# Rows of wo beside the values: sums, parts and loads in another order; one load ahead of stores at the end

## The chip, the cores and the metric

The kernel runs on one core of one Trainium2 chip. The metric is the time of one execution in device microseconds, taken as the median of several runs. A profile is one execution recorded by the hardware profiler; its times are counted from the start of its span. The engines are PE (matmul; its weight loads are PEld), DVE (vector), ACT (scalar), POOL (GpSimd) and SP, which here only issues transfers. An engine works through its instructions in order, and an instruction that waits holds up those behind it on that engine.

## The reference

The output is a blend of two blocks on the same input x of 2048 x 1024, with a gate from x:

```python
g = sigmoid((x * gate_w).sum(-1, keepdims=True))
a = attention(x, wqkv, wo)        # 32 heads of 32, softmax, then @ wo
b = peer(x, w_q, k1, k2, u, v)    # 32 heads; each token's best of 64 experts, gelu, @ v
return g * a + (1 - g) * b
```

Everything is float32.

## The kernel before, in words

The work is one long program in an order written by hand (`manual_schedule`): the tile framework adds the waits that data and buffers need, and nothing is moved. Matrix products of 128x512 are made with operands split into a high and a low part (ACT makes the high part by a copy, DVE the low part by a subtraction; `split`, lines 98 and 99), three matmuls for each product of parts. The large ones save one eighth of the matmuls: a product of 2x2 blocks is made from seven products P1 to P7 of sums of blocks (class `Halves`), whose results DVE adds.

The stages, one after the other: queries and keys (to about 360 us), the router of the second block, the values, attention of 32 heads, and the product with wo. The change touches the seam between values and attention, and the last stage.

**The values.** `values_unit(u)` for u = 0 to 6 makes 256 rows of the values by seven products (line 987), in 19 us. P1 is followed by a copy on ACT; after P6 DVE makes four additions (`combine`, line 916), after P2, P3 and P4 one each. The four sums that come out are stored to the DRAM tensors VD[0] and VD[1] (named vd), from where attention loads its V. While unit u runs, ACT and DVE make all factors of unit u + 1. The products use fixed banks of PSUM. In the last unit the order is P1, P7, P5, P6, P3, P2, P4, and between P2 and P4 PE makes the first eight score matmuls of attention (`first_scores`, line 1278) into the banks 5, 6, 7, 0, 1, 2, 5, 6; bank 2 holds P3 until DVE has added it.

**The rows of wo beside them.** In the units 3 to 6 (i = 0 to 3) four combinations T1 to T4 of blocks of wo are made for the last stage. `load_early(i)` loads four pieces of 128x512 into `early` (named xl in the profile), on POOL's queue. `sums_early` makes the four combinations in place, with four operations on DVE. `split_early(i, j)` makes the parts of combination j (the low part in place) and stores both to TD (t0h, t0l and so on), on POOL's queue. The pieces of i + 1 go into the same places, so a load has to wait until the low part there is stored. Before, the sums came after P7 (k == 1), the parts after P5 (k == 2: j = 0, 1) and after P6 (k == 3: j = 2, 3), each behind that product's own operations, and behind them the four loads.

**The queues.** Transfers are issued by SP, ACT or POOL, whose rows carry the line of the helper `dma` (L80). In the last unit, three of the stores to VD were on SP's queue and one (from P4) on POOL's. Behind them SP issues `load_v`, four transfers that bring V of the first four heads, and then K and Q of head 1.

**Attention.** For every two tiles of keys PE makes eight score matmuls (line 1385) and then two tiles' products with V (line 1406). Z holds K and Q of head 0; two rows of its K are set to 1 by a memset on DVE (line 1293), before in unit 3.

**The last stage.** The first chunk of 256 rows is made plainly (`wo_mm`, line 1622), the others by seven products each, in `unit(n)`. `plain_out` copies the plain chunk's four banks to SBUF and stores them, on SP's queue. `load_t(3, ...)` loads T4, a factor of P4, in eight transfers into the right halves of the tiles woh and wol, also on SP's queue.

Of the kernel before, what the change touches and what calls it, by code (L numbers as in the profile page):

```python
# [17 lines left out]
D = 1024  # L18
H = 32
KC = D // 128  # L20
HC = KC // 2
# [10 lines left out]
def gated_mha_peer_kernel(ctx, tc, xT, wqkv, wv, wo, wq, k12, ug, v, out):  # L32
# [8 lines left out]
    nc = tc.nc  # L41
# [10 lines left out]
    VD = [dram.tile([S, 512], F32, name=f"vd{i}") for i in range(2)]  # L52
# [3 lines left out]
    wo_rows = wo.rearrange("(j d) m -> d j m", j=4)  # L56
# [21 lines left out]
    def dma(dst, src, queue=nc.sync):  # L78
        a, b = (ap.bitcast(F32) if ap.dtype == F32R else ap for ap in (dst, src))
        return queue.dma_start(a, b)  # L80
# [190 lines left out]
    def load_kq(h, tiles):  # L271
        for t, which in zip(tiles, (1, 0)):
            src = QKD[which][32 * h:32 * h + 32]
            dma(t[:32, :], src[:, QK_PARTS[which][0], :])
            dma(t[32:96, :], src.rearrange("d a s -> (d a) s"))

    def load_shift(h, tiles):
        dma(tiles[1][96:98, :], SHD[h])
# [636 lines left out]
    def tt(out, a, b, op=OP.add):  # L915
        nc.vector.tensor_tensor(out=out, in0=a, in1=b, op=op)  # L916
# [12 lines left out]
    def load_x_raw(u):  # L929
        dma(x_raw[u % 2], xT[:, u * W:(u + 1) * W].rearrange("(k p) m -> p k m", p=128))  # L930
# [146 lines left out]
    def peer_turn(Ahl):  # L1077
        for n in range(NQ):
            pt = bank_at((5, 0, 1, 7)[n])
            for t in range(4):  # L1080
                nc.tensor.transpose(pt[:, t * 128:(t + 1) * 128],
                                    Ahl[:, 4 * n + t, :].bitcast(F32), ident)
            at = Z[0][:, n * 512:(n + 1) * 512]
            nc.scalar.activation(at, pt, AF.Copy)
            dma(ATD[:, n * 512:(n + 1) * 512], at)
# [64 lines left out]
    early = more[:, :4]  # L1150
    for k, name in enumerate(("S1", "S3", "th0", "th1")):
        work[name] = more[:, 4 + k]

    def load_early(i):
        for j in range(4):
            c0 = (i + j // 2 * HC) * D + j % 2 * 512
            dma(early[:, j], wo_rows[:, :, c0:c0 + 512], nc.gpsimd)

    def sums_early():
        b11, b12, b21, b22 = (early[:, j] for j in range(4))  # L1160
        tt(b11, b12, b11, OP.subtract)
        tt(b12, b22, b12, OP.subtract)
        tt(b22, b22, b11, OP.subtract)
        tt(b21, b21, b22, OP.subtract)

    def split_early(i, j):
        hi, lo = work[f"th{j}"].bitcast(F32R), early[:, j].bitcast(F32R)
        split(hi, lo, early[:, j])
        for part, t in enumerate((hi, lo)):

            dma(TD[(0, 2, 3, 1)[j]][part][:, i, :], t, nc.gpsimd)

    load_early(0)
    NU = (NT - 2) // 2
    pso = None
    peer = {}
# [10 lines left out]
    def values_unit(u):  # L1187
        last = u == NU - 1
        c1, u2, u3, u5 = (work[k] for k in ("c1", "u2", "u3", "u5"))
        if last:  # L1190
            free = x_raw[(u + 1) % 2].rearrange("p k m -> p (k m)").rearrange("p (a m) -> p a m", m=512)
            c1, u2, u3, u5 = (free[:, k] for k in range(4))
        order = (("P1", "P2", "P3", "P7", "P5", "P6", "P4") if u == 0 else
                 ("P1", "P7", "P5", "P6", "P3", "P2", "P4") if last else
                 ("P1", "P7", "P5", "P6", "P2", "P3", "P4"))
        bank_no[0] = 6 if u else 7
        p, done = {}, set()

        def out(j, half, t, queue=nc.sync):
            dma(VD[half][(2 * u + j) * 128:(2 * u + j + 1) * 128, :], t, queue)  # L1200

        def combine(name):
            if name == "P6":
                tt(u2, c1, p["P6"])
                tt(u3, u2, p["P7"])
                tt(u2, u2, p["P5"])
                tt(u5, u3, p["P5"])
                out(1, 1, u5)
            if "P6" in p:
                if "P2" in p and "C11" not in p:  # L1210
                    p["C11"] = tt(c1, c1, p["P2"])
                    out(0, 0, c1)
                if "P3" in p and "C12" not in p:
                    p["C12"] = tt(u2, u2, p["P3"])
                    out(0, 1, u2)
            if name == "P4":
                tt(u3, u3, p["P4"])

                out(1, 0, u3, nc.gpsimd if last else nc.sync)

        for k, name in enumerate(order):
            if last and name == "P4":

                nonlocal pso
                ps1.close()
                pso = Pool("pso", space=PSUM, side="right")
            p[name] = hv.product(name, bank=pv_bank if last and name == "P4" else None)
            if last and name == "P2":
                first_scores((5, 6, 7, 0), (1, 2, 5, 6))
            if name == "P1":  # L1230
                nc.scalar.activation(c1, p[name], AF.Copy)
                hv.rows(x_raw[(u + 1) % 2])
                if u + 2 < NU:
                    load_x_raw(u + 2)
            combine(name)

            if u + 1 < NU:
                if k == (4 if u == 0 else 0):
                    hv.parts("A11")
                    for s in ("S3", "S1", "S2", "S4"):  # L1240
                        hv.sums(s)
                    done = {"P1"}
                if k >= 4 or u > 0:
                    for q in ("P7", "P5", "P6", "P2", "P3", "P4"):
                        if q in p and q not in done and (k != 4 or u > 0 or q in ("P7", "P5")):
                            hv.parts(hv.FACTORS[q][0])
                            done.add(q)
            for f in ASIDE.get((u, k), ()):
                f()
            if u >= NU - HC:  # L1250
                i = u - NU + HC
                if k == 1:
                    sums_early()
                for j in {2: (0, 1), 3: (2, 3)}.get(k, ()):
                    split_early(i, j)
                if k == 3 and not last:
                    load_early(i + 1)

    P, pools = {}, {}

# [7 lines left out]
    def first_scores(*banks):  # L1268

        tp.close()  # L1270
        pools.update(right=Pool("ppr", side="right"), next=0)
        K, Q = Z
        for kt, places in enumerate(banks):
            pt = p_tile(0, kt)
            for qc, i in enumerate(places):
                ps = ps1.tile([128, 512], F32, name=f"bk{i}")
                c = slice(qc * 512, (qc + 1) * 512)
                nc.tensor.matmul(ps, K[:98, kt * 128:(kt + 1) * 128], Q[:98, c], start=True, stop=True)
                nc.scalar.activation(pt[:, c], ps, AF.Exp, scale=SCALE)
# [4 lines left out]
    for u in range(NU):  # L1284
        values_unit(u)
        if u == 2:
            peer_turn(peer["Ahl"])
            for i in range(2):
                Z[i] = zp.tile([128, S], F32R, name=f"z{i}")
            load_kq(0, Z)  # L1290
            load_shift(0, Z)
        if u == 3:
            nc.vector.memset(Z[0][96:98, :].bitcast(F32), 1.0)
    xw.close()
    vw.close()
# [246 lines left out]
    for h in range(H):  # L1542
        base = h * NT
        g, j = divmod(h, 4)
# [62 lines left out]
    woh, wol = {}, {}  # L1607
# [5 lines left out]
    def load_at(n):  # L1613
        AT[n] = fin.tile([128, W], F32R, name="at", bufs=3)
        dma(AT[n], ATD[:, n * W:(n + 1) * W])
# [45 lines left out]
    def load_t(i, *parts):  # L1661

        ops = ht.b.setdefault(f"T{i + 1}", [None, None])
        for n, (part, src) in enumerate(zip(parts, TD[i])):
            if part is None:
                continue
            m = HC // len(part)
            for j, place in enumerate(part):
                dma(place, src[:, m * j:m * j + m, :].rearrange("p k m -> p (k m)"))
            ops[n] = [place[:, k * 512:(k + 1) * 512] for place in part for k in range(m)]  # L1670
# [10 lines left out]
    def plain_out(n, pa):  # L1681
        for i, ((j, half), ps) in enumerate(pa.items()):
            if i % 2:
                nc.scalar.activation(post[:, i], ps, AF.Copy)
            else:
                nc.vector.tensor_copy(post[:, i], ps)
            store(n, j, half, post[:, i])
# [54 lines left out]
    early = ht.product("P1"), ht.product("P7")  # L1742
    wo_mm(pa, 0, [KC - 1], False, True)
    scale_o(1, 1)
    for name in ("A12", "S1"):
        ht.operand(name)
    load_at(2)
    plain_out(0, pa)
    load_t(3, *([part[k][:, 512:] for k in range(HC)] for part in (woh, wol)))
    ht.places(zp.tile([128, S], F32R, name="z0"), "S2")  # L1750
    ht.places(wk.tile([128, S], F32R, name="acc0", bufs=1), "S4", "A22")

# [124 lines left out]
```

## Time and profile before

| what | us |
|---|---|
| median of three runs (1792.36, 1794.11, 1793.98) | 1793.98 |
| the profiled execution | 1792.93 |
| its span | 1791.1 |
| PE busy | 1785.0 |
| DVE busy | 1512.5 |
| ACT busy | 1309.3 |
| POOL busy | 276.7 |

The span runs from the first to the last instruction; 1.83 us of the profiled execution lie outside it. In a row of the timeline stand the start, the length, the engine, the line, the operation, what it writes and reads, and how many are merged; a bracket gives the idle time before it and what ended that. A matmul's end is modelled, and PE can be slower than at its best while it counts as busy. Rows of transfers stand for their issue; when the data has landed is in the view of the transfers, or in the chain of waits as a piece marked DMA.

### The profile page before, as it was taken

The numbers are of one execution on the slowest core, as the hardware profiler recorded it, in microseconds if no ns is written. First come the engines' busy times: TensorE is split into PE (matmuls) and PEld (weight loads), VectorE is DVE, ScalarE is ACT, GpSimd is POOL, SyncE is SP. The second block draws the span as 40 slices with busy tenths as digits, with TensorE's granted clock in tenths as the row PEclk, the third lists the DMA queues.
The fourth block names the chain that finished last, engine by engine and source line by source line (L and its number), as shares of the span: only waits on it lengthen the run. The fifth ranks groups of instructions, "written<-read, shape, count | busy, mean of one in ns | idle before, by whom it ended". The sixth has DMA issues, their size and how long they took to land.

```text
span 1791.1 us, 26113 instructions
## 1 busy us (share of the span) xinstructions
PE 1785.0 (100%) x9895; PEld 1091.3 (61%) x9895; DVE 1512.5 (84%) x1307; ACT 1309.3 (73%) x1710; POOL 276.7 (15%) x412
## 2 busy tenths in 40 slices
PE   9999999999999999999999999999999999999999
PEld 7777777888888644444444444444444444447887
DVE  8866876779988798989899899989989898887874
ACT  6545544532443599999999999999999999994221
POOL 1222222244203201111110111111110111000000
PEclk9999999999999999999999999999999999999999
DMA  7887687361347769789889988988988897888641
GB/s 291 311 308 270 225 311 291 132 215 46 122 171 260 234 137 210 174 188 197 169 196 194 206 183 203 198 189 188 195 202 185 181 204 168 202 190 278 226 159 59
DMA packets 119975, 361.17 MB, mean 202 GB/s; under 512 B 17416, under 2 KB 51480, under 8 KB 97128
## 3 DMA queue, kind: packets, MB, share of 16 engines
q0 software_dynamic: 30800, 156.82, 37.9%
q1 hardware_dynamic: 88272, 201.48, 35.5%
q8 instruction: 78, 1.28, 0.3%
q10 hardware_dynamic: 776, 1.19, 0.2%
q14 instruction: 49, 0.40, 0.1%
HBM read 173.04 MB, written 72.36 MB: 137 GB/s over the span
## 4 chain that ended last, share of the span: by engine, by line
PE 91%; issue 3%; DMA 3%; DVE 2%; POOL 0%; ACT 0%; SPq 0%; POOLq 0%; DVEq 0%; ACTq 0%
PE ring L1385 29%; PE o L1406 26%; PE bk L304 15%; PE pa L987 7%; PE bk L729 5%; PE bk L292 2%; PE bk L346 2%; PE bk L1003 1%; PE bk L987 1%; DMA xl<-in_wo 1%; PE pa L1629 1%; PE ring L1419 0%; PE bk L194 0%; DMA rb<-rd 0%; DVE xh L916 0%
## 5 line engine op out<-in xcount | busy, mean ns | idle before, releaser
L1395 ACT ACTIVATE P<-ring 128x1024 f32<-128x1024 f32 (+2 forms) x1029 | 910.4, 984 | 17.3 <-PE ring L1385 1.4
L1435 DVE TENSOR_TENSOR acc<-acc,P 128x2048 f32<-128x2048 f32 x230 | 527.0, 2291 | 34.8 <-ACT P L1395 14.6
L1406 PE MATMUL o<-P,V 128*32 128x512 f32 x3840 | 464.8, 599 | 0.6 <-DMA V<-vd 0.6
L1385 PE MATMUL ring<-Q,K 98*128 98x512 f32 x1024 | 272.4, 408 | 0.0
L1385 PEld LDWEIGHTS ring<-Q,K 98*128 98x128 f32 x1024 | 182.1, 188 | 144.5 <-ACT P L1395 82.7
L1385 PE MATMUL ring<-z,z 98*128 98x512 f32 x1016 | 269.5, 407 | 0.0
L1385 PEld LDWEIGHTS ring<-z,z 98*128 98x128 f32 x1016 | 180.8, 188 | 141.7 <-ACT P L1395 77.5
L1435 DVE TENSOR_TENSOR vhl<-vhl,P 128x2048 f32<-128x2048 f32 x104 | 238.3, 2291 | 17.4 <-ACT P L1395 8.5
L1406 PEld LDWEIGHTS o<-P,V 128*32 128x32 f32 x3840 | 98.9, 109 | 223.6 <-issue 214.3
L1428 POOL DMA_DIRECT2D accd<-P x81 | 71.9, 887 | 819.1 <-ACT P L1395 474.1
L304 PE MATMUL bk<-xh,A 128*128 128x512 f32 x336 | 81.9, 394 | 0.0
L304 PE MATMUL bk<-xh,S 128*128 128x512 f32 x336 | 81.0, 392 | 0.0
L304 PE MATMUL bk<-xl,S 128*128 128x512 f32 x336 | 79.7, 389 | 0.0
L1433 DVE TENSOR_TENSOR acc<-P,P 128x2048 f32<-128x2048 f32 x22 | 50.4, 2293 | 31.6 <-ACT P L1395 31.6
L304 PEld LDWEIGHTS bk<-xh,A 128*128 128x128 f32 x336 | 62.2, 188 | 22.0 <-issue 2.5
L139 ACT ACTIVATE hi<-u 128x512 fp32r<-128x512 f32 x42 | 26.6, 632 | 65.5 <-DVE u L520 35.7
L304 PEld LDWEIGHTS bk<-xl,S 128*128 128x128 f32 x336 | 63.0, 188 | 13.1
L304 PEld LDWEIGHTS bk<-xh,S 128*128 128x128 f32 x336 | 62.6, 188 | 12.9
L987 PE MATMUL pa<-woh,acc 128*128 128x512 f32 x216 | 70.0, 389 | 0.0
L1395 ACT ACTIVATE accd<-ring 128x1024 f32<-128x1024 f32 (+2 forms) x64 | 62.2, 1031 | 0.7 <-PE ring L1385 0.6
L520 DVE TENSOR_TENSOR u<-u,bk 128x512 f32<-128x512 f32 x70 | 46.6, 682 | 5.7 <-DMA wpd<-u 5.0
L1438 DVE TENSOR_TENSOR acc<-acc,accd 128x2048 f32<-128x2048 f32 x22 | 50.3, 2285 | 0.0
(323 smaller groups left out, 2305.4 us busy)
## 6 DMA issues: line engine op xcount, KB each, us to landing
accd<-P POOLq DMA_DIRECT2D x81, 1024.0 KB, 9.8
wqt<-in_wq SPq DMA_DIRECT2D x48, 512.0 KB
wraw<-in_wqkv SPq DMA_DIRECT2D x28, 512.0 KB
acc<-acc POOLq DMA_DIRECT2D x19, 512.0 KB, 11.8
kd<-hi POOLq DMA_DIRECT2D x32, 256.0 KB, 3.3
kd<-lo POOLq DMA_DIRECT2D x32, 256.0 KB, 5.3
qd<-hi POOLq DMA_DIRECT2D x32, 256.0 KB, 3.5
qd<-lo POOLq DMA_DIRECT2D x32, 256.0 KB, 3.5
```

The source lines that it names most:

```text
L292: nc.tensor.matmul(b0[w, n], AW[PLAIN[w, ki]][a][:, k, :], X[f"B{ki + 1}{n + 1}"][b][:, k, :], start=first, stop=last)
L304: nc.tensor.matmul(ps, a[i][:, k, :], b[j][:, k, :], start=(k == 0 and i == j == 0), stop=(k == HC - 1 and i == 1))
L520: nc.vector.tensor_tensor(out=out, in0=a, in1=b, op=OP.add)
L729: nc.tensor.matmul(ps, x_part(a, t // 4, kc)[:, tok], b, start=first, stop=last)
L987: nc.tensor.matmul(ps, self.a[a][i][:, k, :], self.b[b][j][k], start=(not first and k == 0 and i == j == 0), stop=(k == HC - 1 and i == 1))
L1385: on_ring(nc.tensor.matmul(ring[:, i, :], K[:98, kt * 128:(kt + 1) * 128], Q[:98, qc * 512:(qc + 1) * 512], start=True, stop=True), i)
L1395: on_ring(nc.scalar.activation(P[h, kt][:, q0 * 512:(q0 + m) * 512].rearrange("p (a m) -> p a m", a=m), ring[:, i:i + m, :], AF.Exp, scale ...
L1406: nc.tensor.matmul(O[h][32 * qc:32 * qc + 32, :], Vt[g][:, kt, 32 * j:32 * j + 32], p[:, qc * 512:(qc + 1) * 512], start=(kt == 0), stop=( ...
L1428: nc.gpsimd.dma_start(ACCD[h], P[h, kt], accum_op=OP.add)
L1433: nc.vector.tensor_add(ACC[h], P[h, 0], P[h, kt])
L1435: nc.vector.tensor_add(ACC[h], ACC[h], P[h, kt])
L1438: nc.vector.tensor_add(ACC[h], ACC[h], ACCD[h])
```

## The change

Nothing is computed otherwise. Five things move:

- In the units 3 to 6 the sums come after P1 (k == 0), the parts all after P7 (k == 1).
- The next unit's pieces of wo are loaded one by one, between the stores of the parts: piece 0 behind the stores of j = 1, piece 1 behind those of j = 2, pieces 2 and 3 behind those of j = 3.
- In the last unit all four stores to VD are on POOL's queue.
- The memset of two rows of K stands after unit 5 instead of unit 3.
- `load_t(3, ...)` stands ahead of `plain_out`.

```diff
-    def load_early(i):
-        for j in range(4):
-            c0 = (i + j // 2 * HC) * D + j % 2 * 512
-            dma(early[:, j], wo_rows[:, :, c0:c0 + 512], nc.gpsimd)
+    def load_early(i, j):
+        c0 = (i + j // 2 * HC) * D + j % 2 * 512
+        dma(early[:, j], wo_rows[:, :, c0:c0 + 512], nc.gpsimd)
...
-        def out(j, half, t, queue=nc.sync):
-            dma(VD[half][(2 * u + j) * 128:(2 * u + j + 1) * 128, :], t, queue)
+        def out(j, half, t):
+            dma(VD[half][(2 * u + j) * 128:(2 * u + j + 1) * 128, :], t, nc.gpsimd if last else nc.sync)
...
-            if u >= NU - HC:
+            if u >= NU - HC and k < 2:
                 i = u - NU + HC
-                if k == 1:
+                if k == 0:
                     sums_early()
-                for j in {2: (0, 1), 3: (2, 3)}.get(k, ()):
+                for j in range(4) if k == 1 else ():
                     split_early(i, j)
-                if k == 3 and not last:
-                    load_early(i + 1)
+                    if j > 0 and not last:
+                        load_early(i + 1, j - 1)
+                        if j == 3:
+                            load_early(i + 1, j)
...
-        if u == 3:
+        if u == NU - 2:
             nc.vector.memset(Z[0][96:98, :].bitcast(F32), 1.0)
...
     load_at(2)
+    load_t(3, *([part[k][:, 512:] for k in range(HC)] for part in (woh, wol)))
     plain_out(0, pa)
-    load_t(3, *([part[k][:, 512:] for k in range(HC)] for part in (woh, wol)))
```

On POOL, in one of the units 3 to 5, the parts' stores (t0h to t3l) and the loads of wo (xl from in_wo) stood like this before:

```order
L80 DMA t0h<-xl_4464 128x512
L80 DMA t0l<-xl_4464 128x512
L80 DMA t2h<-xl_4464 128x512
L80 DMA t2l<-xl_4464 128x512
L80 DMA t3h<-xu 128x512
L80 DMA t3l<-xl_4464 128x512
L80 DMA t1h<-xu 128x512
L80 DMA t1l<-xl_4464 128x512
L80 DMA xl_4464<-in_wo 128x1x512 x4
```

After the change, on POOL in the same unit:

```order
L80 DMA t0h<-xl_4464 128x512
L80 DMA t0l<-xl_4464 128x512
L80 DMA t2h<-xl_4464 128x512
L80 DMA t2l<-xl_4464 128x512
L80 DMA xl_4464<-in_wo 128x1x512
L80 DMA t3h<-xu 128x512
L80 DMA t3l<-xl_4464 128x512
L80 DMA xl_4464<-in_wo 128x1x512
L80 DMA t1h<-xu 128x512
L80 DMA t1l<-xl_4464 128x512
L80 DMA xl_4464<-in_wo 128x1x512 x2
```

Two loads have moved in between the stores; each stands behind the store of the low part in its own place.

On DVE, in the last unit, the sums and low parts of wo (xl, xu) stood around the additions of P6 (four, from the banks bk_5394, bk_5356 and bk_5373), P3 (bk_5420) and P2 (bk_5435) before:

```order
L916 TENSOR_TENSOR xl_4464<-xl_4464 128x512 x4
L99 TENSOR_TENSOR xl_4464<-xl_4464 128x512 x2
L916 TENSOR_TENSOR xh_4449<-xh_4449,bk_5394 128x512
L916 TENSOR_TENSOR xh_4449<-xh_4449,bk_5356 128x512
L916 TENSOR_TENSOR xh_4449<-xh_4449,bk_5373 128x512 x2
L99 TENSOR_TENSOR xl_4464<-xl_4464,xu 128x512 x2
L916 TENSOR_TENSOR xh_4449<-xh_4449,bk_5420 128x512
L916 TENSOR_TENSOR xh_4449<-xh_4449,bk_5435 128x512
```

After the change, on DVE in the last unit, where the three banks of P6's additions are called bk_5402, bk_5360 and bk_5389, and z_4897 is K of head 0:

```order
L1295 MEMSET z_4897 2x2048
L916 TENSOR_TENSOR xl_4464<-xl_4464 128x512 x4
L99 TENSOR_TENSOR xl_4464<-xl_4464 128x512 x2
L99 TENSOR_TENSOR xl_4464<-xl_4464,xu 128x512 x2
L916 TENSOR_TENSOR xh_4449<-xh_4449,bk_5402 128x512
L916 TENSOR_TENSOR xh_4449<-xh_4449,bk_5360 128x512
L916 TENSOR_TENSOR xh_4449<-xh_4449,bk_5389 128x512 x2
L916 TENSOR_TENSOR xh_4449<-xh_4449,bk_5420 128x512
L916 TENSOR_TENSOR xh_4449<-xh_4449,bk_5435 128x512
```

The second pair of low parts has moved ahead of P6's additions, and the memset ahead of the sums.

On SP, at the end of the values, the stores to vd, the load of V and the first of K (minus: only before):

```order
 L80 DMA vd_66<-xh_4449 128x512
 L80 DMA vd_65<-xh_4449 128x512
-L80 DMA vd_66<-xh_4449 128x512 x2
-L80 DMA vd_65<-xh_4449 128x512
 L80 DMA V<-vd_65 128x4x128 x4
 L80 DMA K_5533<-kd 32x2048
```

The three stores of the last unit that stood ahead of V's load on SP have gone to POOL, where they stand behind the last parts' stores.

More of the change, by code (lines that the diff above doesn't have):

```diff
@@ L1171, in split_early @@
             dma(TD[(0, 2, 3, 1)[j]][part][:, i, :], t, nc.gpsimd)
-    load_early(0)
+    for j in range(4):
+        load_early(0, j)
     NU = (NT - 2) // 2
@@ L1217, in combine @@
                 tt(u3, u3, p["P4"])
-                out(1, 0, u3, nc.gpsimd if last else nc.sync)
+                out(1, 0, u3)
         for k, name in enumerate(order):
```

## The prediction, made before the changed kernel was run

> **What bounds the kernel now.** I read the page first, then the waits of PE, then PE's busy time by stretches. From the page and from the waits of PE (who waited for what: us in total, times, longest):
>
> ```profile
> span 1791.1 us, 26113 instructions
> PE 1785.0 (100%) x9895; PEld 1091.3 (61%) x9895; DVE 1512.5 (84%) x1307; ACT 1309.3 (73%) x1710; POOL 276.7 (15%) x412
> ```
>
> ```profile
> PE bk L420 <- DVE ones L75: 1.1, 1, 1.1
> PE o L1406 <- DMA V<-vd: 0.6, 1, 0.6
> PE bk L1278 <- DVE xh L916: 0.6, 1, 0.6
> PE bk L729 <- ACT xu L733: 0.3, 1, 0.3
> PE pa L1622 <- ACT z L98: 0.2, 1, 0.2
> ```
>
> PE is busy for 1785.0 of 1791.1 us, and its recorded waits add up to 2.8 us, in five places. A reordering of transfers and vector work that leaves the matmuls alone can win back no more than such waits, plus what a matmul loses while it already counts as busy. Two of the five, 0.6 us each, lie where the change works, at the seam between the values and attention. PE's busy time in the last values unit and in attention (us of the stretch, then PE busy, then the other engines):
>
> ```profile
> 585.30:604.30 19.00, 18.42 (x82) 14.92 (x81) 12.31 (x20) 5.93 (x11) 7.56 (x15) 1.00 0.66 235
> 632.00:1600.00 968.00, 968.00 (x5971) 454.14 (x5973) 873.66 (x397) 948.85 (x1094) 114.72 (x134) 1.00 0.85 189
> ```
>
> Attention has no gap in 968 us, so a start that is earlier by some time is carried to its end, and nothing can be won inside it. The seam on PE, in order of time (start, us, what, and in brackets the idle time before it with its releaser):
>
> ```profile
> 598.82 2.88 PE L987 MATMUL bk<-xl,a 128*128 128x512 f32 x12
> 601.54 1.33 PE L1278 MATMUL bk<-z,z 98*128 98x512 f32 x5
> 603.45 0.96 PE L1278 MATMUL bk<-z,z 98*128 98x512 f32 x3 [0.58 <-DVE xh L916]
> 604.24 2.90 PE L987 MATMUL o<-xl,vo 128*128 128x512 f32 x12
> 609.57 1.92 PE L1406 MATMUL o<-P,V 128*32 128x512 f32 x16 [0.59 <-DMA V<-vd]
> ```
>
> The first row is P2, the last product before the early scores (L1278). The sixth score matmul goes into the bank of P3, and waits 0.58 us until DVE has added P3 out of it. At 609.57 the first product with V waits 0.59 us for V's load. Together that is 1.17 us.
>
> **The rows of wo and the wait for P3's bank.** DVE in the last two units, with the memset that the change moves:
>
> ```profile
> 549.24 1.76 DVE L1293 MEMSET z<- 2x2048 f32 x1 [0.48 <-issue]
> 576.68 2.14 DVE L916 TENSOR_TENSOR xl<-xl 128x512 f32<-128x512 f32 x3 [0.66 <-DMA xl<-in_wo]
> 593.78 0.69 DVE L916 TENSOR_TENSOR xl<-xl 128x512 f32<-128x512 f32 x1 [5.11 <-DMA xl<-in_wo]
> 595.61 2.15 DVE L916 TENSOR_TENSOR xl<-xl 128x512 f32<-128x512 f32 x3 [1.13 <-DMA xl<-in_wo]
> 597.67 1.28 DVE L99 TENSOR_TENSOR xl<-xl 128x512 fp32r<-128x512 f32 x2
> 598.87 2.72 DVE L916 TENSOR_TENSOR xh<-xh,bk 128x512 f32<-128x512 f32 x4
> 601.51 1.29 DVE L99 TENSOR_TENSOR xl<-xl,xu 128x512 fp32r<-128x512 f32 x2
> 602.71 1.28 DVE L916 TENSOR_TENSOR xh<-xh,bk 128x512 f32<-128x512 f32 x2
> ```
>
> In the last unit the sums wait 5.11 and 1.13 us for wo's pieces; from 595.61 on DVE runs without a gap: three sums, two low parts, the four additions of P6, two low parts, P3. P3's addition ends near 603.39 (half of the last row), and PE goes on at 603.45. After the change the same operations precede it; the two later low parts only move ahead of the four additions. So the order within DVE buys this bank nothing: P3 still comes out some 7.8 us (603.39 - 595.61) after the last of wo's pieces has landed. What can buy it is an earlier landing. PE would have wanted the bank at 603.45 - 0.58 = 602.87, so the piece has to land about 0.6 us earlier.
>
> POOL issues the parts' stores and the next loads; first its rows in the unit before, then from the chain of waits the load that came last, and from the view of the DMAs around it two median times to landing (the last number):
>
> ```profile
> 580.32 0.55 POOL L80 DMA_DIRECT2D t0l<-xl  x1 [2.75 <-DVE xl L99]
> 585.83 0.54 POOL L80 DMA_DIRECT2D t1l<-xl  x1
> 589.93 0.54 POOL L80 DMA_DIRECT2D xl<-in_wo  x1 [1.73 <-DMA t1l<-xl]
> ```
>
> ```profile
> 589.93 5.58 DMA xl<-in_wo
> t0l<-xl POOLq DMA_DIRECT2D x4, 256.0 KB, 2.4
> t1l<-xl POOLq DMA_DIRECT2D x4, 256.0 KB, 3.9
> ```
>
> The last load may only start once the low part that lies in its place has been stored: issued 585.83, landed 3.9 to 4.1 us later. That store waits for the last low part, which today stands behind the four additions of P6; these take 2.64 us (601.51 - 598.87, the same block as in the last unit). With the parts directly behind each other the store, and with it the load, could go up to 2.6 us earlier. Against that stands the new order on POOL: each load now stands between stores, and while POOL waits for a low part's landing, the later stores wait behind it. I count from t0l. It goes 0.6 to 1.3 us earlier than 580.32, since S1's low part (half of the 1.28 us of a pair) no longer stands ahead of it on DVE and the 0.66 us of waiting may go. Then come its landing, 2.4, and five issues of 0.54 (a load, t3h, t3l, a load, t1h): t1l is issued at 584.1 to 584.8 instead of 585.83, so the last load goes 1.0 to 1.7 us earlier, near 588.5. Its landing, 5.58 us today with three other loads just ahead, should take no longer, since the four no longer start together. The need is 0.6 us, so I take the whole wait: **-0.58**. By the bounds on the load (0 and 2.6 us earlier) the term lies between 0 and -0.58; what would put it above 0 is rival (d).
>
> In units 3 to 5 the same moves cost PE nothing. All factors are made one unit, 19 us, ahead of the product that reads them, and PE shows no wait there. What now stands behind the sums' wait for wo (0.66 us at 576.68) is S3's low part, and it is read only by P7 of the next unit. The memset takes 1.76 us out of unit 3 and puts it ahead of the last unit's sums, where DVE idles 5.11 us; without that cover it would delay P3 by the same 1.76 us.
>
> **The last unit's stores, and V.** SP's own queue:
>
> ```profile
> 564.54 39.80 SPq L80 DMA_DIRECT2D vd<-xh  x11
> 604.43 7.69 SPq L80 DMA_DIRECT2D V<-vd  x4
> 612.17 1.07 SPq L80 DMA_DIRECT2D K<-kd  x2
> ```
>
> V's first load is issued at 604.43, right behind the last of the eleven stores, which waits for DVE's addition of P2. The first V product starts 609.57 - 604.43 = 5.14 us later. Three stores leave this queue for POOL's. In the changed program's list V's first load then waits for nothing later than PE's product P2, which ends near 601.7. At the same 5.14 us V is there at 606.8, while PE would come to it at 609.57 - 0.59 - 0.58 = 608.40 at the earliest. The margin is 1.6 us: **-0.59**, bounds 0 and -0.59. Only the fourth piece of V holds rows of the last unit; it waits for the last store, which was on POOL already, and K of the next head behind it stays at about 612 and is wanted only when head 0 is through (a head takes about 31 us: 968 us for the 31 heads in that stretch).
>
> What the three stores cost on POOL, from the operations on that tensor (ns min/median/max):
>
> ```profile
> L80 SPq DMA_DIRECT2D vd<-xh x11: 319/320/320, 564.5 to 604.0; - x11
> L80 POOL DMA_DIRECT2D vd<-xh x1: 543/543/543, 608.2 to 608.2; - x1
> ```
>
> An issue takes 543 ns there instead of 320, so 3 x 0.22 = 0.67 us more in all, on an engine that is 15% busy and that nobody waits for: 0. [...] Were all of it in V's path, the sum would be 0.67 us worse.
>
> **The fourth combination.** SP's rows at the end, and the only wait for a transfer that PE's weight loads have there:
>
> ```profile
> 1644.77 0.42 SPq L80 DMA_DIRECT2D at<-atd  x1
> 1649.73 1.88 SPq L80 DMA_DIRECT2D out<-rb  x4
> 1651.69 1.87 SPq L80 DMA_DIRECT2D woh<-t3h  x4
> 1653.61 2.15 SPq L80 DMA_DIRECT2D wol<-t3l  x4
> ```
>
> ```profile
> PEld pa L987 <- DMA wol<-t3l: 0.2, 1, 0.2
> ```
>
> The stores wait for the plain chunk's copies until 1649.73, and the eight loads go behind them; the weights of P4 come so late that a weight load waits 0.2 us. Put ahead, the loads start near 1645.2 and take about 4 us to issue, so the stores go out within about 1 us of 1649.73, and nothing is late. I take **-0.1**, bounds 0 and -0.2, since a weight load's wait is partly covered by the matmul before it.
>
> **Sum.** -0.58 - 0.59 - 0.10 = -1.27 us: span 1791.1 becomes 1789.8. The profiled execution took 1792.93 us, 1.05 below the median of 1793.98; it would take 1791.7, and the median would be 1792.7.
>
> **The rivals.**
> (a) V comes no sooner: its transfer shares the 16 DMA engines with the last unit's stores, and takes over 6.7 us (608.4 - 601.7) instead of 5.14. For it: those stores and wo's parts are in flight then. Against it: the parts go out earlier after the change. It keeps 0.59: 1793.98 - 0.68 = 1793.3. [...]
> (b) The last piece of wo lands no sooner, as POOL's new waits eat what the parts win: the 0.58 stays, and it is 1793.3 again. Against it: 0.6 of the 1.0 to 1.7 us suffices.
> (c) The head start is given back: the chain behind the last head, whose last wait is the 0.2 at L1622, is a row of transfers that does not move. Against it: it starts from the last exponentials, which follow PE. No change: 1794.0.
> (d) Slower: POOL's waits between the stores put off the last load, or it lands late. From the operations on that tile:
>
> ```profile
> DMA to landing us min/median/max: 2.3/3.9/8.2
> ```
>
> Issued at 589.93 as now and landing after 8.2 us rather than 5.58, it comes 2.6 us later, and PE waits 0.58 + 2.6 = 3.2 us; with V and P4 gained, that is +1.9: 1795.9. It decides from a landing after 595.5; to lose over 0.2% it would take one more such wait.
>
> **How the numbers follow.** 0.2% is 3.6 us, about what a measurement of this kernel can tell from no change. Forecast 0.64, (a) 0.10, (b) 0.10, (c) 0.07, (d) 0.06, of which a good half over 0.2%; 0.03 for a gain that no row shows. So faster 0.03, same 0.93, slower 0.04. The runs shown spread from 1792.36 to 1794.11. The low end is the lowest run less 1.27 and less the 0.2 at L1622 too, rounded down: 1790.8. The high end is (c) with 1.0 for such a spread: 1795.0. Only (d) and the unseen gain lie outside.
>
> **What would show it.** Right: PE's waits for DVE at L1280 and for V at L1408 are gone; V's first load is issued near 601.7; wo's last load of the unit before the last is issued near 588.5; PE's wait at L1624 stays near 0.2; no wait for wol<-t3l. Wrong: a score wait above 0.6 us, V's first load still at 604, or a span above 1792.

## The result, and the profile after

The changed kernel is slower: 1804.99 us in the median of 6 runs (1802.57 to 1805.15) against 1794.05 for the kernel before (6 runs, 1792.36 to 1795.14). The ratio is 1.0062, with a 95% interval of 1.0051 to 1.0073. The forecast was 1792.7, so it missed by 12.3 us, in sign and in size. The profiled execution took 1805.15 us, 12.2 more than that of before.

The page of the changed kernel, and the waits of PE (us in total, times, longest; from L1280 on the lines of the code are two further down than before; two waits far from the change, 1.1 and 0.3 us, are left out):

```profile
span 1803.3 us, 26111 instructions
PE 1789.6 (99%) x9895; PEld 1092.7 (61%) x9895; DVE 1512.5 (84%) x1307; ACT 1308.2 (73%) x1710; POOL 277.9 (15%) x415
```

```profile
PE bk L1280 <- DVE xh L916: 3.2, 2, 2.3
PE ring L1387 <- ACT P L1397: 2.0, 3, 1.0
PE pa L987 <- ACT acc L98: 1.8, 1, 1.8
PE pa L987 <- DVE rb L916: 1.6, 1, 1.6
...
PE pa L987 <- DVE acc L99: 0.3, 1, 0.3
```

All waits add up to 10.3 us instead of 2.8, and PE counts as busy 4.6 us longer with the same 9895 matmuls. Together that is 12.1 of the span's 12.2. The wait for V is gone, as forecast, and so is the wait for wol; the scores' wait has grown from 0.6 to 3.2, and three waits in the last stage are new.

The seam on PE after the change:

```profile
601.79 0.63 PE L1280 MATMUL bk<-z,z 98*128 98x512 f32 x2
604.75 0.50 PE L1280 MATMUL bk<-z,z 98*128 98x512 f32 x1 [2.34 <-DVE xh L916]
606.07 2.50 PE L1280 MATMUL bk<-z,z 98*128 98x512 f32 x5 [0.82 <-DVE xh L916]
608.37 3.41 PE L987 MATMUL o<-xl,vo 128*128 128x512 f32 x12
613.55 1.92 PE L1408 MATMUL o<-P,V 128*32 128x512 f32 x16
```

Now the third score waits already, for a bank of P6, and then the fourth. Behind the waits five scores take 2.50 us, where five took 1.33 before, and P4 takes 3.41 instead of 2.90. The same matmuls are slower there because the granted clock was halved, 0.50 instead of 1.00. In the windows of the changed kernel (stretch, its length, PE busy, the other engines, and in the third number from the end the granted clock):

```profile
602.61:606.02 3.41, 0.50 (x1) 0.19 (x1) 3.34 (x7) 1.29 (x3) 2.99 (x6) 1.00 0.80 256
606.02:609.43 3.41, 3.36 (x8) 2.68 (x9) 1.19 (x2) 2.53 (x5) 1.62 (x3) 0.50 1.06 402
1667.57:1670.98 3.41, 1.58 (x7) 0.79 (x5) 3.13 (x4) 0.63 (x1) 0.00 (x0) 1.00 0.98 399
1670.98:1674.39 3.41, 3.08 (x8) 2.35 (x8) 2.33 (x4) 0.90 (x2) 0.00 (x0) 0.50 0.18 67
```

Two stretches of 3.41 us ran at half clock, one at the seam and one in the last stage; each costs, as an estimate from that clock, up to half its length, 1.7 us. Before, no such stretch lies inside the span. So the first product with V starts at 613.55 instead of 609.57, 3.98 us later: +2.58 by the scores' waits (3.16 less 0.58), +1.7 by the clock, -0.59 by V, and +0.25 that lay ahead of the seam.

What the scores waited for is traced back through DVE to POOL. DVE in the last unit, then POOL in the unit before it and SP's first load of V:

```profile
595.31 0.69 DVE L916 TENSOR_TENSOR xl<-xl 128x512 f32<-128x512 f32 x1
598.82 2.15 DVE L916 TENSOR_TENSOR xl<-xl 128x512 f32<-128x512 f32 x3 [2.82 <-DMA xl<-in_wo]
603.30 3.92 DVE L916 TENSOR_TENSOR xh<-xh,bk 128x512 f32<-128x512 f32 x6
```

```profile
584.08 0.55 POOL L80 DMA_DIRECT2D t0l<-xl  x1 [2.12 <-DVE xl L99]
...
586.96 0.54 POOL L80 DMA_DIRECT2D xl<-in_wo  x1 [1.12 <-DMA t0l<-xl]
...
589.62 0.56 POOL L80 DMA_DIRECT2D t1l<-xl  x1
593.13 0.55 POOL L80 DMA_DIRECT2D xl<-in_wo  x1 [2.95 <-DMA t3l<-xl]
595.51 0.54 POOL L80 DMA_DIRECT2D xl<-in_wo  x1 [1.84 <-DMA t1l<-xl]
```

```profile
601.98 1.66 SPq L80 DMA_DIRECT2D V<-vd  x3
```

The last load of wo goes at 595.51 instead of 589.93, 5.58 us later. It lands faster than before, so its piece comes 3.2 us later, and the last three sums start at 598.82 instead of 595.61 (from the chain of waits; before, the landing took 5.58):

```profile
595.51 3.21 DMA xl<-in_wo
```

The additions that give the banks free, P6's four, P2's and P3's, are one block from 603.30 on. V's load goes at 601.98 instead of 604.43.

T0's low part is late already, at 584.08 instead of 580.32. What is late ahead of it is not a piece of wo: the unit's sums start at 579.72 and wait for none. The chain of waits leads from them to ACT, whose copy of P1 (line 1231) writes into the tile `c1` (xh in the rows), and to the store that still reads `c1`, that of the sum with P2 from the unit before:

```profile
569.63 5.57 DMA vd<-xh
...
575.30 0.60 ACT L1231 ACTIVATE xh<-bk 128x512 f32<-128x512 f32 x1 [8.21 <-DMA vd<-xh]
...
579.72 2.86 DVE L916 TENSOR_TENSOR xl<-xl 128x512 f32<-128x512 f32 x4
```

Before, this store went at 566.94 and took 3.27 us, and the copy came at 570.31. Late pieces come in one unit earlier: in unit 4 the last three sums waited 4.61 us for wo, 1.91 before, and on DVE the additions that end with this store stand behind them.

The last stage: SP's row of the plain chunk's stores, then the piece of the chain of waits that ends in the loss, then DVE, ACT and PE in order:

```profile
1660.82 2.22 SPq L80 DMA_DIRECT2D out<-rb  x4
```

```profile
1652.58 10.06 DMA woh<-t3h
...
1662.71 5.05 DMA out<-rb
```

```profile
1667.85 0.69 DVE L916 TENSOR_TENSOR rb<-osb,pa 128x512 f32<-128x512 f32 x1 [6.35 <-DMA out<-rb]
...
1669.71 0.63 ACT L98 ACTIVATE acc<-V 128x512 fp32r<-128x512 f32 x1 [9.01 <-DVE V L1678]
1670.39 0.50 PE L987 MATMUL pa<-woh,acc 128*128 128x512 f32 x1 [1.83 <-ACT acc L98]
```

The plain chunk's last store goes out only when a load of T4 has landed, and lands itself 5.05 us later. The stores do not read T4; the trace shows what they wait for. SP's transfers carry eight semaphores in turn there: T4's loads from 1651.04 on have the numbers 105, 106, 108, 109, 110, 100, 102 and 104, and the four stores behind them 105, 106, 108 and 109 again, those of the four loads of woh eight places ahead. Each store went after a wait for one of these loads, 2.9 us in all. (On POOL's queue the third store to vd in the last unit waits 0.53 us for t2h in the same way, eight places ahead; both carry number 116.) SP's waits for woh (us in total, times, longest):

```profile
SPq L80 <- DMA woh<-t3h: 2.9, 4, 2.2
```

On DVE an addition waits 6.35 us for the landing of the last store: it is the first unit's addition of P2, which writes into `post[:, 3]`, the tile that this store reads. Behind it in DVE's order stand the scaling (line 1678) and the parts of the next unit's factors. PE waits for these and for a later addition behind them: 1.83 + 0.33 + 1.57 us, and 1.7, by the estimate above, by the half clock.

Of the 12.2 us, 3.98 arise at the seam; the first products with wo behind attention are 6.48 later (1636.44 against 1629.96 for the same block), so 2.5 arise in attention, and the last 5.7 in the last stage.

### The profile page after: what moved, and what is told of

Same layout as the page of the kernel before. It is cut to its first block, busy times and chain, and to the rows that moved or that the text cites. A ratio compares the mean times of both kernels' runs of the same rounds, so it can differ in the third digit from the quotient of the medians.

```text
span 1803.3 us, 26111 instructions
## 1 busy us (share of the span) xinstructions
PE 1789.6 (99%) x9895; PEld 1092.7 (61%) x9895; DVE 1512.5 (84%) x1307; ACT 1308.2 (73%) x1710; POOL 277.9 (15%) x415
## 4 chain that ended last, share of the span: by engine, by line
PE 93%; DMA 3%; issue 2%; DVE 1%; ACT 0%; POOL 0%; POOLq 0%; DVEq 0%; ACTq 0%; SPq 0%
PE ring L1387 27%; PE o L1408 25%; PE bk L304 15%; PE pa L987 7%; PE bk L987 5%; PE bk L729 5%; PE bk L292 2%; PE bk L346 2%; DMA accd<-P 2%; PE bk L1003 1%; PE pa L1624 1%; PE pa L1631 1%; DMA woh<-t3h 1%; PE ring L1421 0%; PE bk L194 0%
```

## The experiments

Theory I says that the loads of wo between the stores are what makes the seam late; theory S, that the last stage is late because the addition of P2 reuses the tile of a store which T4's loads hold back. Each run is compared with the kernel before on the same chip: 1793.79 us for the first four, 1793.34 for the next four, 1792.62 for the last two.

**1. T4's loads back behind the stores** (the changed kernel with one move undone).

```diff
-    load_t(3, *([part[k][:, 512:] for k in range(HC)] for part in (woh, wol)))
     plain_out(0, pa)
+    load_t(3, *([part[k][:, 512:] for k in range(HC)] for part in (woh, wol)))
```

> The changed kernel with T4's eight loads back behind the plain chunk's stores. Theory S (the stores that T4's loads put off are waited for by DVE before it may write P2's sum of chunk 1 into their buffer; PE then waits 3.7 us and runs 3.4 us at half clock): the last stage loses its 5.4 us, about 1799.5, and PE has no wait at L987 at the end. Rival (the last stage is late because of what came before it, whatever the order of T4's loads): 1804 to 1805.

Measured: 1798.15 us (10 runs, 1796.83 to 1799.56), ratio 1.0024 (1.0015 to 1.0034). No wait of PE is left in the last stage, and the scores still wait:

```profile
PE bk L1280 <- DVE xh L916: 3.7, 2, 2.9
```

The mean granted clock is 0.998 or 0.999 in all ten runs, against 1.0 in the runs of the kernel before: a half clock has stayed, and the scores' 3.7 us of waits put it at the seam. Without the move of T4's loads 4.4 of the 11 us are left.

**2. That move alone** (the kernel before).

```diff
+    load_t(3, *([part[k][:, 512:] for k in range(HC)] for part in (woh, wol)))
     plain_out(0, pa)
-    load_t(3, *([part[k][:, 512:] for k in range(HC)] for part in (woh, wol)))
```

> The kernel before with T4's eight loads ahead of the plain chunk's stores and nothing else. Theory S: the same waits of DVE and PE as in the changed kernel, 1794 + 5.4 = 1799.5. Rival (the move is harmless by itself, as forecast): 1793.9 to 1794.

Measured: 1798.54 us (11 runs, 1796.57 to 1804.17), ratio 1.0028 (1.0019 to 1.0037). The longest of PE's waits in the last stage, and DVE's row:

```profile
PE pa L987 <- DVE rb L916: 2.9, 1, 2.9
```

```profile
1661.54 0.69 DVE L916 TENSOR_TENSOR rb<-osb,pa 128x512 f32<-128x512 f32 x1 [6.11 <-DMA out<-rb]
```

It needs nothing else of the change: alone it costs 4.75 us. In eight of the eleven runs the mean clock is below 1.0, though not in the profiled one.

**3. The four loads together again, behind all stores** (the changed kernel).

```diff
-                    if j > 0 and not last:
-                        load_early(i + 1, j - 1)
-                        if j == 3:
-                            load_early(i + 1, j)
+                    if j == 3 and not last:
+                        for q in range(4):
+                            load_early(i + 1, q)
```

> The changed kernel, sums after P1 and parts after P7, but the four loads of the next unit behind all eight stores, as before. Theory I (loads between the stores lengthen the landing of the low parts' stores behind them, on the same queue, and so put off the last load): the last load of unit 5 goes back from 595.5 to about 588, the score waits of 3.2 us and the half clock behind them go, about 1800.5. Rival Q (sums first on DVE put the units' own additions behind wo's landing, and the delay feeds itself from unit to unit): the last load stays at 594 or later, 1804 to 1805.

Measured: 1798.79 us (11 runs, 1796.02 to 1802.27), ratio 1.0028 (1.0019 to 1.0037). T0's low part, its last load and the scores' wait:

```profile
582.49 0.55 POOL L80 DMA_DIRECT2D t0l<-xl  x1 [2.12 <-DVE xl L99]
...
590.01 0.54 POOL L80 DMA_DIRECT2D xl<-in_wo  x1 [1.03 <-DMA t1l<-xl]
```

```profile
PE bk L1279 <- DVE xh L916: 0.8, 1, 0.8
```

The seam is nearly as before the change, though sums and parts are still early. So the loads' place is the cause there, not the order on DVE alone. From T0's low part to the last load it takes 7.52 us here, 9.61 before and 11.43 in the changed kernel. But T0's low part is 2.17 us later than before here too, and the last load comes at 590.01 where 588 was expected: ACT's copy of P1 again waits for the store from `c1`, 6.49 us.

**4. A tile of its own for the addition of P2** (the changed kernel; T4's loads stay ahead).

```diff
-            r = post[:, 3] if n == 1 else c1
+            r = osb() if n == 1 else c1
```

> The changed kernel, in which P2's sum of chunk 1 goes to a tile of its own, not into the buffer of the plain chunk's fourth store; T4's loads stay ahead. Theory S: DVE's 6.4 us wait for the store is gone, and with it PE's waits and half clock at the end: about 1799.5. Rival (the loads of chunk 3, behind the late stores, are late too and PE waits for them): 1803 to 1805.

Measured: 1797.81 us (9 runs, 1796.54 to 1800.33), ratio 1.0023 (1.0014 to 1.0033). SP's stores go out late all the same; the addition no longer waits, and PE has no wait in the last stage:

```profile
1659.27 3.62 SPq L80 DMA_DIRECT2D out<-rb  x4
```

```profile
1660.91 0.68 DVE L916 TENSOR_TENSOR osb<-osb,pa 128x512 f32<-128x512 f32 x1
```

Late stores are harmless here; what costs is that a tile is written again which such a store reads.

**5. Both causes off** (the edits of 3 and 4 in the changed kernel).

> The changed kernel with both suspected causes taken off at once: wo's four loads behind all of the parts' stores again, and the eleventh addition of the end's first unit writes into a tile of its own. What stays of the change: sums and parts in their new places, the memset, the three stores on POOL, T4 ahead of the plain chunk's stores. Theory of two causes (the loads between the stores, and the reuse of the fourth store's tile, are the whole loss): the loss is gone, 1792.0 to 1794.2 beside the kernel before; the scores wait at most 0.8 us for DVE's addition of P3, PE waits for nothing at the end, and no record of the half clock lies inside the span. Rival, a third cause (the new places of sums and parts, or slower landings in attention that the change brings): 1795.5 or more, with a shift of over 1.5 us that grows inside attention.

Measured: 1792.02 us (11 runs, 1791.41 to 1796.13), ratio 0.9999 (0.9990 to 1.0008). The whole loss is gone; by the interval, what is left of the change costs no more than 1.4 us in all, so no third cause shows. Against the kernel before, the change costs 10.9 us, without the one cause 5.0 (experiment 3), without the other 4.0 (experiment 4), without both -1.3: singly they take off 5.9 and 6.9 us, together 12.3. T0's low part and POOL's last load:

```profile
580.57 0.55 POOL L80 DMA_DIRECT2D t0l<-xl  x1 [2.12 <-DVE xl L99]
...
588.09 0.54 POOL L80 DMA_DIRECT2D xl<-in_wo  x1 [1.03 <-DMA t1l<-xl]
```

Between the two lie 7.52 us again. Up to the last stage this is the code of experiment 3, so the 1.92 us between their last loads are scatter from one execution to another. No score and no V product waits, and the first product with V starts 1.38 us sooner than before (608.19 against 609.57). Nine of the eleven runs lie between 1791.41 and 1793.83, the two others at 1796.1 with a mean clock of 0.999. It beats the changed kernel; that it beats the kernel before, as its median would have it, the interval does not show.

**6. The three stores on POOL alone** (the kernel before; SP keeps no store of the last unit).

```diff
-        def out(j, half, t, queue=nc.sync):
-            dma(VD[half][(2 * u + j) * 128:(2 * u + j + 1) * 128, :], t, queue)
+        def out(j, half, t):
+            dma(VD[half][(2 * u + j) * 128:(2 * u + j + 1) * 128, :], t, nc.gpsimd if last else nc.sync)
...
-                out(1, 0, u3, nc.gpsimd if last else nc.sync)
+                out(1, 0, u3)
```

> The kernel before with the three stores of the last values unit on POOL's queue, and nothing else. My term for V (-0.59): 1793.2, PE's wait for V is gone and V's first load is issued near 601.9 instead of 604.43, while the scores' wait of 0.58 stays. Rival, the gain is taken back by a later wait or V lands later: no change, 1793.8, or 1794.5 and more if POOL's longer issues or the parts' stores ahead of them hold V's fourth piece back.

Measured: 1793.53 us (11 runs, 1792.27 to 1795.35), ratio 1.0003 (0.9994 to 1.0012). SP's load of V and PE's first product with V:

```profile
602.01 11.30 SPq L80 DMA_DIRECT2D V<-vd  x4
```

```profile
608.99 1.92 PE L1406 MATMUL o<-P,V 128*32 128x512 f32 x16
```

V's load goes 2.42 us sooner, its wait is gone, and attention begins 0.58 us earlier. In the total this is too little to be seen.

**7. The loads between the stores alone** (the kernel before, with sums and parts where they were, and `load_early(i, j)` for one piece as in the changed kernel).

```diff
                     split_early(i, j)
-                if k == 3 and not last:
-                    load_early(i + 1)
+                    if j > 0 and not last:
+                        load_early(i + 1, j - 1)
+                        if j == 3:
+                            load_early(i + 1, j)
```

> The kernel before, with only wo's loads moved in between the parts' stores as in the changed kernel (sums, parts, memset, stores and T4 where they were). Theory of the loads between the stores: POOL's waits for landings put the last load of the unit before the last off by 3 to 6 us (from 589.93 to 593 or later), the sums land late, the scores wait 3 to 6 us for P3's addition and a record of the half clock of 3.4 us follows: 1796.5 to 1800. Rival, the loads harm only together with the earlier sums and parts: the last load within 1.5 us of 589.93, 1793.5 to 1795.

Measured: 1796.02 us (11 runs, 1794.27 to 1798.96), ratio 1.0017 (1.0008 to 1.0026). POOL, and PE's waits:

```profile
582.06 0.55 POOL L80 DMA_DIRECT2D t0l<-xl  x1 [2.12 <-DVE xl L99]
...
593.85 0.54 POOL L80 DMA_DIRECT2D xl<-in_wo  x1 [1.75 <-DMA t1l<-xl]
```

```profile
PE bk L1280 <- DVE xh L916: 1.5, 2, 1.1
```

The last load is 3.92 us later than before: 11.79 us behind T0's low part instead of 9.61, which is 2.18, and T0's low part itself is 1.74 later. The sign is as theory I had it, the size less: 1.5 us of waits where 3 to 6 were expected, and no half clock in the profiled run, which is the fastest of the eleven; in nine of them the mean clock is below 1.0. With sums and parts early too (the changed kernel, experiments 1 and 4) the scores wait 2.9 to 3.7 us. There T0's low part is later still (584.08 to 585.20), and so is the landing of the last piece: 598.73 in the changed kernel against 597.07 here, 1.66 later, as much as the scores wait longer (3.16 against 1.5). One reason is in the order on DVE: with all four low parts ahead of P6's additions, the store from `c1` in unit 4 goes at 569.63 instead of 568.51 here, and its landing took 5.57 us instead of 4.07. How much of the 1.66 each of these made was not taken apart.

**8. The parts that gain, alone** (the kernel before with the stores of experiment 6, T4's loads ahead, and the tile of experiment 4).

> The kernel before with the three stores on POOL, T4's loads ahead of the plain chunk's stores, and a tile of its own for the eleventh addition of the end's first unit. Theory of two causes: V's wait of 0.59 and the last weight wait are gone and nothing is late at the end: 1792.3 to 1793.3, a little below the kernel before, by less than a measurement can tell. Rival, T4's loads ahead harm also by another way (the stores' landings compete, the copies' tiles come free late): 1795 or more, with a wait of PE at the end.

Measured: 1792.93 us (11 runs, 1791.44 to 1796.10), ratio 1.0000 (0.9991 to 1.0009). No wait for V or wol, none of PE in the last stage. As the theory of two causes has it, a little less in the median, and not to be told from no change. The first product with V starts at 608.18, as early as in experiment 5 although sums and parts stand in their old places.

**9 and 10. What a wait of PE costs beyond its length** (the kernel before, with one, then four, operations on DVE ahead of P3's addition in the last unit; they change no value).

```diff
+                    for _ in range(1 if last else 0):
+                        tt(u2, u2, u2, OP.max)
                     p["C12"] = tt(u2, u2, p["P3"])
```

> A probe of what a wait of PE costs beyond its own length: the kernel before with one more operation on DVE ahead of P3's addition in the last values unit (the maximum of a 128x512 tile with itself, which changes no value, some 0.7 us). The sixth score waits 0.58 + 0.7 = 1.3 us. [...]

> The same probe with four such operations: the sixth score waits 0.58 + 2.8 = 3.4 us. Theory of the clock's windows: at least half of some window is idle in nearly every run, and the 3.41 us behind it are at half clock, which costs up to 1.7 us more: a mean granted clock of 0.999 in nearly all runs and 1793.34 + 2.8 + 1.2 to 1.7 = 1797.3 to 1797.8. Rival, only the wait itself: 1796.1, and a clock of 1.0.

Measured for one: 1794.56 us (11 runs, 1792.09 to 1797.86), ratio 1.0008 (0.9999 to 1.0017). The wait was 1.64 us, not 1.3, and the profiled run has a stretch of 3.41 us at half clock; the mean clock was below 1.0 in 3 of the 11 runs. For four: 1798.00 us (7 runs, 1797.18 to 1799.59), ratio 1.0030 (1.0018 to 1.0041), with a wait of 3.39 us and a mean clock of 0.998 or 0.999 in all seven. The windows, cut where the granted clock changes, first of the short probe, then of the long one:

```profile
602.64:606.05 3.41, 1.77 (x8) 1.14 (x7) 2.83 (x5) 2.89 (x6) 1.60 (x3) 1.00 0.85 333
606.05:609.46 3.41, 3.41 (x9) 2.62 (x8) 0.00 (x0) 1.10 (x3) 0.00 (x0) 0.50 1.04 323
```

```profile
602.27:605.68 3.41, 0.58 (x3) 0.14 (x1) 3.20 (x6) 2.24 (x5) 1.61 (x3) 1.00 0.83 327
605.68:609.09 3.41, 2.85 (x7) 2.27 (x8) 1.10 (x2) 1.57 (x3) 0.00 (x0) 0.50 0.56 186
609.09:612.51 3.42, 3.42 (x10) 2.65 (x9) 0.00 (x0) 0.00 (x0) 0.00 (x0) 0.50 0.69 198
```

The long wait is 2.8 us longer than that of before and costs 5.4 us in the median, where the rival (only the wait) had 2.8 and the theory 4.0 to 4.5: the rival falls. In the profiled execution the first product with V starts at 614.59, 5.02 us later than before, so the cost arises at this place. The theory lacked the second stretch at half clock, which followed the first here.

## Why the prediction was wrong, point by point

- **"so the last load goes 1.0 to 1.7 us earlier, near 588.5"** is the step that failed at the seam: 595.51, some 7 us later than that. Most of it, 4.4 to 5.1 us, lies in the count's start: T0's low part was to go 0.6 to 1.3 us earlier than 580.32 and went at 584.08. The count looked at DVE's order in this unit alone; the delay came from the unit before, by way of the store from `c1` and ACT's copy. Even with the loads behind the stores T0's low part was not earlier (582.49 and 580.57 in the experiments 3 and 5); in experiment 3 the store from `c1` took 6.61 us to land, against 3.27 before. Why it lands later once sums and parts are early stays open. Another 2.2 us lie behind it: from T0's low part to the last load 9.2 us were counted (5.1 to t1l, then 4.1 for its landing) and 11.43 measured, most of it because t1l now landed after 5.6 us. The landing of the load itself was to take no longer than 5.58 us, and took 3.21. That "in units 3 to 5 the same moves cost PE nothing" was true of PE and still misled.
- **The term of -0.58** became +2.58 and a half clock. That parts directly behind each other bring the last load nearer was right: 7.52 us behind T0's low part in the experiments 3 and 5 instead of 9.61. The loads between them took more than that away. The size of the term rested on one execution: experiment 2, with the code of before up to the last stage, has no wait of the scores at all.
- **"so the stores go out within about 1 us of 1649.73, and nothing is late"** is the step that failed in the last stage, and dearer: experiment 2 has +4.75 us for it alone. The count took the loads' issue alone, about 4 us; the stores also wait for the landing of the loads eight places ahead, and went at 1653.02 and later there. That these late stores would make nothing else late was assumed: a later writer of one of their four tiles had not been looked for. The expected gain itself, the wait for wol, did come.
- **The term of -0.59 for V** was right: 601.98 was forecast as near 601.7, and the wait is gone in the changed kernel and in experiment 6. Rival (a) fell.
- **Rival (d)** named the mechanism at the seam, and its 3.2 us of waits were measured as 3.16. That agreement is in part luck: it was priced as a load issued on time that lands 2.6 us later, where the load went 5.58 us later and landed 2.4 us faster. It had no line for the clock, and none for the last stage. Rivals (b) and (c) would have left the time about where it was, so they do not bear on this result.
- **The memset** cost nothing that shows: it ends at 595.28, and the last three sums wait until 598.82 for a piece of wo.
- **Attention** was to carry the start through unchanged. It added 2.5 us in the profiled execution; PE's 2.0 us of waits for exponentials there go with ACT's waits for a landing of accd (3.2 us in three places, 0.5 in one before). Nothing in the change touches these transfers, and the experiments 5 and 8, with the same code in attention, are as fast as the kernel before, though experiment 8 has 3.1 us of the same waits of ACT. Why they landed late in that execution stays open.

## What to carry to other kernels

A transfer that must wait for another's landing belongs, by these runs, at the end of its queue's group: with nothing but the loads put between the stores (experiment 7) the last load went 11.79 us behind T0's low part instead of 9.61, and in the changed kernel the delay was handed from unit 4, where the sums waited 4.61 us for wo instead of 1.91, to unit 5, where T0's low part went 3.76 us later. Before a load is moved ahead of stores, find out whose landing each store will then wait for, and look up every later writer of the tiles that those stores read, and what stands behind that writer on its engine. Both losses here ran through such a writer: ACT's copy into `c1` at the seam, DVE's addition into `post[:, 3]` at the end. Price a wait of PE not by its length alone, but also by the half clock that may follow: in experiment 10 a wait 2.8 us longer cost 5.4 us.

## What the runs showed of the hardware that was not expected

In the changed kernel and in experiments 3, 9 and 10 the half clock came in stretches of 3.41 us. In the windows of that length read at the seam and in the last stage, one at half clock followed where PE had been busy for 0.50 us (the changed kernel, from 602.61), 1.58 (the same, from 1667.57), 0.76 (experiment 3), 1.77 (experiment 9) and 0.58 us (experiment 10). None followed where it had been busy for 1.84 (the changed kernel, from 1674.39), 1.98, 1.87 or 2.03 us (experiment 2), nor at the very end of experiment 3, for 1.71 us; the ends of matmuls are modelled. The same wait came with and without it: PE waits 2.92 us for DVE in the last stage of the experiments 2 and 3. In experiment 2 the wait lies across two windows, in experiment 3 mostly in one; first experiment 2, then experiment 3:

```profile
1665.84:1669.25 3.41, 1.87 (x9) 1.20 (x7) 2.07 (x4) 1.16 (x2) 0.00 (x0) 1.00 0.03 12
1669.25:1672.66 3.41, 2.03 (x9) 1.74 (x10) 3.08 (x5) 0.14 (x1) 0.00 (x0) 1.00 0.00 0
```

```profile
1669.05:1672.46 3.41, 0.76 (x4) 0.30 (x2) 2.60 (x5) 0.63 (x1) 0.00 (x0) 1.00 0.01 2
1672.46:1675.87 3.41, 3.14 (x8) 2.49 (x9) 2.60 (x5) 1.15 (x2) 0.00 (x0) 0.50 0.00 0
```

A low part's store also landed later with a load just ahead of it in its queue. In the units 4 and 5 t1l took 5.0 to 6.1 us in the four kernels with the loads between the stores (the changed one, experiments 1, 4 and 7), and 3.7 to 4.1 in all others. Experiment 3 (4.0 and 3.9) differs from the changed kernel (5.5 and 5.6) in the place of the loads alone.
